# A gated FFT mixer with a token MLP: another order of token loads, layer-norm factors and sines at the start

## The chip, the cores and the metric

The kernel runs on one core of a Trainium2 chip. The metric is device time in microseconds of one execution. The core has a matrix engine (TensorE, PE in the profile), a vector engine (VectorE, DVE), a scalar engine (ScalarE, ACT), GpSimd (POOL) and a queue engine (SyncE, SP) that here only issues transfers. Each of them works through its own instructions in the order in which they were written.

## The reference

Two branches over 2048 tokens of 512 features are mixed by a gate per token.

```python
def _A_ref(x, w_r, w_i):                      # spectral branch
    X = rfft2(x.astype(float32), axes=(-2, -1)) * (w_r + 1j * w_i)
    return irfft2(X, s=(S, D), axes=(-2, -1)).astype(bfloat16)

def _B_ref(x, w1, b1, w2, b2):                # MLP over the tokens
    h = _layernorm(x, axis=-1)
    u = gelu(einsum("bsd,sf->bdf", h, w1) + b1)     # 2048 tokens -> 1792
    return (einsum("bdf,fs->bds", u, w2) + b2).transpose(0, 2, 1)

g = sigmoid((x * gate_w).sum(-1, keepdims=True))
return g * _A_ref(x, ...) + (1 - g) * _B_ref(x, ...)
```

All inputs are bf16. Both branches read the same x.

## The kernel before, in words

The tokens lie in 16 blocks of 128 (one token of a block per partition). `load_x` (line 89) brings blocks of x into `xa` and `xb`, `load_w1a` (line 92) the matching 128 rows of the first 1024 columns of w1 into `w1a`. Both are issued on SP, in the order written in lines 118 to 142. The program has eight semaphores for such transfers and takes them in turn, so that an issue waits until the transfer eight before it has landed.

The layer norm of a block needs its mean and variance. `bstat` (line 245) makes the statistics of one block on VectorE, `bn_aggr` the mean and variance `mv`. For blocks 0 and 1 the factor `rstd` comes from a square root on ScalarE (line 299) and a reciprocal on VectorE (line 302). For the others `aggr` (line 251) adds the epsilon on VectorE or on GpSimd and raises to the power of -0.5 on GpSimd (line 258). Blocks 0 to 5 are normalized on VectorE (`norm_dve`, line 270). Blocks 6 to 15 are normalized on ScalarE in pairs (`norm`, line 260), with the product of mean and factor, `nmr`, made before on VectorE (blocks 6, 7, 14, 15) or GpSimd (the others). The normalized blocks are `hn`.

TensorE first runs eight dummy matmuls on a tile of zeros (line 240). Then it takes the blocks in order: `mm1` (line 274) multiplies block b of `w1a` with block b of `hn` for eight column tiles of w1, and sums over b in eight banks. The first twelve blocks go block by block, the last four column tile by column tile, and a `gelu` on ScalarE follows each finished column tile. After that `products` (line 453) yields the remaining matmuls of the MLP one by one: the other six column tiles of w1 (line 458) and the second product with w2 (line 468). The transforms of the spectral branch (`token`, `dpass`, `inverse`) are put between them; the functions `fill`, `fill_to` and `spent` place them by a written clock in us (`T_TA` = 42.7 and so on, line 24).

The transforms need tables of sines. VectorE and ScalarE make the angles (`md`, `ma`, `mc`), VectorE masks them to a power of two (`mask`, `angles_a`), ScalarE takes the sines (`sines_d`, `sines_a`) into `TD` and `TA`, and two transposing transfers on SP make `TI` and `TB` of them. `gprod` (line 278) multiplies x with the gate weights on VectorE, and `gacc` sums the products on ScalarE. Functions that ScalarE takes from different tables (square root, sine, gelu) need a table load between them, and a one-element activation into `sink` pulls such a load forward.

The order of the norms and of the sines on each engine is that of the loops in lines 296 to 334.

Of the kernel before, what the change touches and what calls it, by code (L numbers as in the profile page):

```python
# [12 lines left out]
F32 = mybir.dt.float32  # L13
I32 = mybir.dt.int32

P = 128
S = 2048
D = 512
NB = 16
# [3 lines left out]
NDVE = 6  # L23
# [20 lines left out]
def kernel(  # L44
# [13 lines left out]
    nc = tc.nc  # L58
# [5 lines left out]
    small = ctx.enter_context(tc.tile_pool(name="small", bufs=1))  # L64
# [3 lines left out]
    def H(i, shape, name, dt=BF16):  # L68
        return big.tile(shape, dt, tag=f"h{i}", name=name)
# [11 lines left out]
    xv = A_x[0].rearrange("(b a) d -> a b d", a=P)  # L81
    w1v = B_w1.rearrange("(b a) f -> a b f", a=P)
    w2v = B_w2.rearrange("(ft f) s -> f ft s", f=P)
    xh = [H(0, [P, 8, D], "xa"), H(1, [P, 8, D], "xb")]
# [4 lines left out]
    def load_x(b0, b1):  # L89
        nc.sync.dma_start(out=xh[b0 // 8][:, b0 % 8:(b1 - 1) % 8 + 1], in_=xv[:, b0:b1])  # L90

    def load_w1a(b0, b1):
        nc.sync.dma_start(out=w1a[b0 // 4][:, b0 % 4:(b1 - 1) % 4 + 1], in_=w1v[:, b0:b1, 0:FT1 * P])
# [8 lines left out]
    def gather_w(i):  # L102
        w = (A_w_r, A_w_i)[i]
        for o, src, idx in ((wn[:, i, 8:16].rearrange("p e l -> p (e l)"), w.rearrange("(c e) l -> c (e l)", e=8), 0),
                            (wn[:, i, 16], w, 1)):
            nc.gpsimd.indirect_dma_start(out=o, out_offset=None, in_=src,
                                         in_offset=bass.IndirectOffsetOnAxis(ap=widx[:, idx:idx + 1], axis=0))
# [13 lines left out]
    nc.scalar.dma_start(out=brow[:], in_=B_b1.rearrange("(ft f) -> ft f", f=P))  # L121
    load_w1a(0, 1)
    load_x(1, 2)
    for b in range(1, 3):
        load_x(b + 1, b + 2)
        load_w1a(b, b + 1)
    load_x(4, 6)
    load_w1a(3, 4)
    load_x(6, 8)
    load_w1a(4, 6)  # L130
    load_x(8, 12)
    load_w1a(6, 8)
    load_x(12, 16)
    load_w1a(8, 12)
    gwb = small.tile([P, D], BF16, name="gwb")
    nc.sync.dma_start(out=gwb[:], in_=gate_w[None, :].to_broadcast([P, D]))
    nc.sync.dma_start(out=brow2[:], in_=B_b2.rearrange("(b a) -> b a", a=P))
# [21 lines left out]
    def iota(dst, pattern, base, cm=0):  # L159
        nc.gpsimd.iota(dst, pattern=pattern, base=base, channel_multiplier=cm,  # L160
                       allow_small_or_imprecise_dtypes=True)
# [19 lines left out]
    def gather_rows():  # L181
        gp = nc.gpsimd
        iota(widx[:, 0:1], [[0, 1]], 255, -2)
        gp.tensor_scalar(wf[:, 0:1], acol[:, 0:1], 63.5, 1016.0, op0=Alu.is_ge, op1=Alu.mult)
        gp.tensor_scalar(wf[:, 1:2], acol[:, 0:1], 0.5, -1024.0, op0=Alu.is_lt, op1=Alu.mult)
        gp.tensor_scalar(wf[:, 2:3], acol[:, 0:1], -16.0, 2048.0, op0=Alu.mult, op1=Alu.add)
        gp.tensor_add(wf[:, 0:1], wf[:, 0:1], wf[:, 1:2])
        gp.tensor_add(wf[:, 0:1], wf[:, 0:1], wf[:, 2:3])
        gp.tensor_copy(widx[:, 1:2], wf[:, 0:1])
# [4 lines left out]
    def mask(m, n):  # L194
        nc.vector.tensor_single_scalar(m, m, n - 1, op=Alu.bitwise_and)

    def nsin(dst, m, n):
        nc.scalar.activation(dst, m, ActF.Sin, bias=c_mpi, scale=2.0 * PI_IN / n)

    def psin(dst, m, n):  # L200
        nc.scalar.activation(dst, m, ActF.Sin, bias=c_pi, scale=-2.0 * PI_IN / n)
# [5 lines left out]
    def sines_d():  # L207
        nsin(TD[:, :, 1], md[:, 1], 1024)
        nsin(TD[:, :, 2], md[:, 0], 1024)
        psin(TD[:, :, 0], md[:, 0], 1024)  # L210

    def angles_a(v):
        mask(ma[v][:], 2048)
        if v == 0:
            mask(mc[:], 2048)

    def sines_a(v):
        if v == 1:
            nsin(TA[:, :, 1], ma[1][:], 2048)
        else:  # L220
            nsin(TA[:, :, 2], ma[0][:], 2048)
            psin(TA[:, :, 0], ma[0][:], 2048)
            nsin(TA[:, 0, 2, 0:1], mc[:], 2048)
            psin(TA[:, 0, 0, 0:1], mc[:], 2048)


    stats = small.tile([P, NB, nc.vector.BN_STATS_DIM], F32, name="stats")
    mv = small.tile([P, NB, nc.vector.BN_AGGR_DIM], F32, name="mv")
# [16 lines left out]
    def bstat(b):  # L245
        nc.vector.bn_stats(out=stats[:, b, :], in_=xh[b // 8][:, b % 8, :])  # L246

    def on_dve(b):
        return b <= NDVE or b == NB - 2

    def aggr(b0, b1):
        for b in range(b0, b1):
            nc.vector.bn_aggr(out=mv[:, b, :], in_=stats[:, b, :])
        eng = nc.vector if on_dve(b0) else nc.gpsimd
        eng.tensor_scalar(mv[:, b0:b1, 1], mv[:, b0:b1, 1], 1e-5, 0.0, op0=Alu.add, op1=Alu.add)  # L255
        if not on_dve(b0):
            nc.gpsimd.tensor_scalar(nmr[:, b0:b1], mv[:, b0:b1, 0], -1.0, 0.0, op0=Alu.mult, op1=Alu.add)
        nc.gpsimd.tensor_tensor(rstd[:, b0:b1], mv[:, b0:b1, 1], c_mhalf.to_broadcast([P, b1 - b0]), op=Alu.pow)  # L258

    def norm(b0, b1):  # L260
        if not on_dve(b0):
            nc.gpsimd.tensor_mul(nmr[:, b0:b1], nmr[:, b0:b1], rstd[:, b0:b1])
        else:
            nc.vector.scalar_tensor_tensor(nmr[:, b0:b1], mv[:, b0:b1, 0], -1.0, rstd[:, b0:b1],  # L264
                                           op0=Alu.mult, op1=Alu.mult)
        for b in range(b0, b1):
            nc.scalar.activation(hn[:, b, :], xh[b // 8][:, b % 8, :], ActF.Identity,  # L267
                                 bias=nmr[:, b:b + 1], scale=rstd[:, b:b + 1])

    def norm_dve(b):  # L270
        nc.vector.tensor_scalar(hn[:, b, :], xh[0][:, b, :], mv[:, b, 0:1], rstd[:, b:b + 1],
                                op0=Alu.subtract, op1=Alu.mult)
# [5 lines left out]
    def gprod(q):  # L278
        nc.vector.tensor_mul(prod[q // 2][:, 4 * (q % 2):4 * (q % 2) + 4],
                             xh[q // 2][:, 4 * (q % 2):4 * (q % 2) + 4],  # L280
                             gwb[:, None, :].to_broadcast([P, 4, D]))
# [5 lines left out]

    sink = small.tile([P, 1], F32, name="sink")
    nc.scalar.activation(sink[:], consts[:, 5:6], ActF.Sqrt, bias=consts[:, 5:6], scale=1.0)
    for v in range(2):  # L290
        nc.vector.tensor_scalar(md[:, v], lrow[:], acol[:, 1:2], 768.0 * v, op0=Alu.mult, op1=Alu.add)


    bcol = small.tile([P, NFT + NB], F32, name="bcol")
    b1f, b2f = bcol[:, 0:NFT], bcol[:, NFT:]
    for b in range(2):
        bstat(b)
        nc.vector.bn_aggr(out=mv[:, b, :], in_=stats[:, b, :])
        nc.scalar.activation(rstd[:, b:b + 1], mv[:, b, 1:2], ActF.Sqrt, bias=consts[:, 5:6], scale=1.0)
        if b == 0:  # L300
            nc.scalar.copy(b1f, pb[:, 0:NFT])
        nc.vector.reciprocal(rstd[:, b:b + 1], rstd[:, b:b + 1])
        norm_dve(b)
    bstat(2)
    nc.scalar.activation(sink[:], consts[:, 2:3], ActF.Sin, bias=c_mpi, scale=0.0)
    for v in range(2):
        nc.scalar.activation(ma[v][:], krow[:], ActF.Identity, bias=consts[:, 3 + v:4 + v], scale=acol[:, 0:1])
    nc.scalar.activation(mc[:], acol[:, 0:1], ActF.Identity, bias=consts[:, 4:5], scale=1024.0)


    aggr(2, 3)
    for b in range(2, NDVE):
        bstat(b + 1)
        norm_dve(b)
        if b + 1 < NDVE:
            aggr(b + 1, b + 2)
    for b in range(NDVE, NB, 2):
        if b > NDVE:
            bstat(b)
        if b == NDVE + 2:  # L320
            norm(b - 2, b)
            sines_d()
        bstat(b + 1)
        aggr(b, b + 2)
        if b == NDVE:
            mask(md[:], 1024)
        if b == NB - 2:
            angles_a(1)
        if b > NDVE:
            norm(b, b + 2)  # L330
        if b == NB - 6:
            angles_a(0)
            sines_a(0)
    sines_a(1)
    for b in range(12):
        for ft in range(FT1):
            mm1(b, ft)
    for q in range(4):
        gprod(q)
    gather_rows()  # L340
    gather_w(0)
    gather_w(1)
# [4 lines left out]
                                in_=TD[:].rearrange("p s t k -> p (s t k)"))  # L347
    nc.sync.dma_start_transpose(out=TB[:].rearrange("p s t k -> p (s t) k"),
                                in_=TA[:].rearrange("p s t k -> p (s t k)"))
# [445 lines left out]
    b = NB - 1  # L795
# [36 lines left out]
```

## Time and profile before

| what | value |
|---|---|
| median of 3 runs | 129.32 us (128.65, 129.32, 130.08) |
| the profiled execution's own time | 128.63 us |
| its span in the profile | 126.7 us |
| TensorE busy | 122.3 us, 97% |
| VectorE busy | 111.6 us, 88% |
| ScalarE busy | 89.7 us, 71% |
| GpSimd busy | 39.6 us, 31% |
| granted TensorE clock, mean | 0.995 |
| transfers | 24.05 MB, mean 190 GB/s |
| first matmul of the first product | 4.82 us |
| last evacuation on VectorE | 123.37 us |

The span reaches from the program's first instruction to its last one; 1.9 us of the execution's time lie outside it. Busy times are sums over the span. A busy TensorE is not the same as a TensorE at its full rate, since its matmuls overlap in the pipeline: the distance from one matmul's end to the next one's tells the rate.

### The profile page before, as it was taken

The page shows a single profiled execution, that of the slowest core. Times are in us where ns is not written, and L with a number is a line of the kernel's source. Part 1 is how long each engine was busy: PE and PEld are TensorE (multiplying, and loading weights), DVE is VectorE, ACT ScalarE, POOL GpSimd, SP SyncE. Part 2 cuts the span into 40 slices and gives each one's busy share as a digit, 9 for nine tenths or more (in the row PEclk, how much of TensorE's full clock was granted, in tenths as well). Part 3 has the DMA queues.
Part 4 walks back from the last instruction along what each step waited for, and adds up shares of the span by engine and source line. Part 5 has one row for each costly group of instructions (what it writes and reads, how often), then busy time and mean ns, then how long its engine had stood idle before and what let it go on. Part 6 is the DMA issues. An engine that isn't in the chain of part 4 may idle for free.

```text
span 126.7 us, 2074 instructions
## 1 busy us (share of the span) xinstructions
PE 122.3 (97%) x750; PEld 65.2 (51%) x750; DVE 111.6 (88%) x190; ACT 89.7 (71%) x137; POOL 39.6 (31%) x67
## 2 busy tenths in 40 slices
PE   6999999999999999999999999999999999999990
PEld 2244444444444576557764765477644444444480
DVE  4799998999999999999999999999999999993140
ACT  4391299999897699998994799229785599522420
POOL 7133288998887198000040000000000000261200
PEclk9999999999999999999999999999999999999998
DMA  3899999998899999999579206710021101269991
GB/s 95 268 327 379 368 374 352 292 309 262 206 276 121 320 290 293 290 287 291 143 220 294 65 0 190 228 42 0 0 79 50 41 3 41 83 82 201 175 224 29
DMA packets 34635, 24.05 MB, mean 190 GB/s; under 512 B 5536, under 2 KB 32032, under 8 KB 34624
## 3 DMA queue, kind: packets, MB, share of 16 engines
q1 hardware_dynamic: 32516, 21.02, 60.4%
q0 software_dynamic: 1936, 2.76, 13.0%
q8 instruction: 6, 0.10, 0.3%
q10 hardware_dynamic: 172, 0.13, 0.3%
q14 instruction: 5, 0.04, 0.1%
HBM read 19.15 MB, written 3.67 MB: 180 GB/s over the span
## 4 chain that ended last, share of the span: by engine, by line
PE 97%; DVE 0%; issue 0%
PE yb L468 36%; PE u L275 22%; PE u L458 16%; PE ivt L657 5%; PE ivd L673 3%; PE pw L240 3%; PE dp L525 3%; PE yb L800 2%; PE tok L516 2%; PE tok L517 2%; PE ivt L651 0%; PE tok L513 0%; DVE tbv L802 0%; DVE warm L145 0%; PE pb L239 0%
## 5 line engine op out<-in xcount | busy, mean ns | idle before, releaser
L468 PE MATMUL yb<-gl,w2t 128*128 128x512 bf16 x210 | 47.4, 379 | 0.0
L468 PEld LDWEIGHTS <-w2t 128*128 128x128 bf16 x210 | 20.2, 98 | 22.1
L275 PE MATMUL u<-hn,w1a 128*128 128x512 bf16 x128 | 28.5, 385 | 0.0
L458 PE MATMUL u<-hn,w1b 128*128 128x512 bf16 x96 | 23.3, 379 | 0.0
L448 ACT ACTIVATE tbv<-yb,ombb,omg 128x512 bf16<-128x512 f32 x15 | 11.6, 775 | 15.3 <-PE yb L468 15.1
L275 PEld LDWEIGHTS <-w1a 128*128 128x128 bf16 x128 | 12.7, 99 | 15.9 <-issue 1.5
L778 POOL DMA_DIRECT2D out_dram<-ap x3 | 4.0, 1528 | 49.2 <-DVE ap L773 45.3
L458 PEld LDWEIGHTS <-w1b 128*128 128x128 bf16 x96 | 9.0, 98 | 8.0
L286 ACT ACTIVATE junk<-prod 128x512 bf16<-128x512 bf16 x16 | 10.1, 631 | 0.3
L354 ACT ACTIVATE gl<-u,bcol 128x512 bf16<-128x512 f32 x14 | 9.2, 688 | 1.3 <-PE u L458 0.8
L629 ACT CAST R<-ivt 128x1024 bf16<-128x1024 f32 x8 | 7.8, 1038 | 2.3 <-PE ivt L657 2.3
L258 POOL TENSOR_TENSOR rstd<-mv,consts 128x2 f32<-128x2 f32 (+1 forms) x9 | 6.3, 703 | 8.1 <-DVE mv L255 8.0
L629 ACT CAST H<-ivd 128x1024 bf16<-128x1024 f32 x7 | 6.9, 1047 | 0.8 <-PE ivd L673 0.8
L787 DVE TENSOR_TENSOR tbv<-tbv,ap 128x512 bf16<-128x512 bf16 x3 | 1.3, 425 | 5.5 <-ACT tbv L448 5.5
L246 DVE BATCH_NORM_STATS2 stats<-xa 128x6 f32<-128x512 bf16 x8 | 5.5, 686 | 0.5 <-DMA xa<-in_A_x_dram 0.5
L267 ACT ACTIVATE hn<-xb,nmr,rstd 128x512 bf16<-128x512 bf16 x8 | 5.8, 802 | 0.0
L547 DVE TENSOR_TENSOR tatb<-PMA,wn 128x1024 bf16<-128x1024 bf16 x8 | 5.0, 690 | 0.2 <-issue 0.2
L246 DVE BATCH_NORM_STATS2 stats<-xb 128x6 f32<-128x512 bf16 x8 | 5.2, 676 | 0.0
L267 ACT ACTIVATE hn<-xa,nmr,rstd 128x512 bf16<-128x512 bf16 x2 | 1.5, 804 | 5.1 <-DVE nmr L264 5.1
L673 PEld LDWEIGHTS <-R 128*128 128x128 bf16 x64 | 3.8, 98 | 2.5 <-ACT R L629 2.5
L547 DVE TENSOR_TENSOR tatb<-PMB,wn 128x2048 bf16<-128x2048 bf16 x4 | 4.7, 1226 | 0.2
L518 ACT CAST ZA<-tok 128x1024 bf16<-128x1024 f32 x4 | 4.0, 1019 | 1.4 <-PE tok L517 1.3
(198 smaller groups left out, 225.8 us busy)
## 6 DMA issues: line engine op xcount, KB each, us to landing
w2t<-in_B_w_dram SPq DMA_DIRECT2D x8, 896.0 KB, 9.8
w1b<-in_B_w_dram SPq DMA_DIRECT2D x3, 1024.0 KB, 16.3
w1a<-in_B_w_dram SPq DMA_DIRECT2D x2, 1024.0 KB
out_dram<-tbv SPq DMA_DIRECT2D x14, 128.0 KB, 4.0
out_dram<-ap POOLq DMA_DIRECT2D x3, 512.0 KB, 6.8
w1a<-in_B_w_dram SPq DMA_DIRECT2D x4, 256.0 KB, 4.4
w1a<-in_B_w_dram SPq DMA_DIRECT2D x2, 512.0 KB, 8.0
xb<-in_A_x_dram SPq DMA_DIRECT2D x2, 512.0 KB, 7.3
```

Source lines behind the costliest of these rows:

```text
L246: nc.vector.bn_stats(out=stats[:, b, :], in_=xh[b // 8][:, b % 8, :])
L267: nc.scalar.activation(hn[:, b, :], xh[b // 8][:, b % 8, :], ActF.Identity, bias=nmr[:, b:b + 1], scale=rstd[:, b:b + 1])
L275: nc.tensor.matmul(u1[ft], lhsT=w1a[b // 4][:, b % 4, ft * P:(ft + 1) * P], rhs=hn[:, b, :], start=(b == 0), stop=(b == NB - 1))
L286: nc.scalar.activation(junk[:], prod[b // 8][:, b % 8], ActF.Copy, accum_out=glog[:, b:b + 1])
L354: nc.scalar.activation(gl[:, ft, :], src, ActF.Gelu_apprx_tanh, bias=b1f[:, ft:ft + 1], scale=1.0)
L448: nc.scalar.activation(tbv[0][:, b], y[:], ActF.Identity, bias=gate["ombb2"][:, b:b + 1], scale=gate["omg"][:, b:b + 1])
L458: nc.tensor.matmul(u[:], lhsT=w1b[c][:, b, k * P:(k + 1) * P], rhs=hn[:, b, :], start=(b == 0), stop=(b == NB - 1))
L468: nc.tensor.matmul(y[:], lhsT=w2t[b // 2][:, ft, (b % 2) * P:(b % 2 + 1) * P], rhs=gl[:, ft, :], start=(ft == 0), stop=(ft == NFT - 1))
L547: mul(tt[:, i, :, r:r + n], PM[:, 2 * s:2 * s + 2, r:r + n], w[:, None].to_broadcast([P, 2, n, 256]))
L629: nc.scalar.copy(out, pr[:].rearrange("p h n -> p (h n)"))
L657: nc.tensor.matmul(o[:, 2 * v:2 * v + 2], lhsT=UV[:, 2 * v + c, r, par::2], rhs=TB[:, s, c:c + 2], start=(c == 0), stop=(c == 1))
L673: nc.tensor.matmul(pr[:, c, o * P:(o + 1) * P], lhsT=plane(par, cos), rhs=TI[:, lst, t], start=True, stop=True)
```

## The change

It rearranges the first 30 us and leaves the rest as it is.

- Token block 2 is issued on ScalarE's queue, behind the square-root table load. SP's list loses that issue, and from block 4 on weight blocks are issued one by one, and tokens 8 to 11 in two pairs.
- Block 2's factor is made like those of 0 and 1, with the root on ScalarE. The statistics of block 3 are taken in two halves of 256 features into a tile `st3`; the first half stands between block 2's root and its reciprocal.
- Blocks 6 and 7 get their factors one at a time instead of as a pair. Block 7's now goes through GpSimd.
- The norms of 8 and 9 stand ahead of the short sines, and those of 14 and 15 ahead of the long ones; the latter stand behind the first gate product in VectorE's order. The mask of `md` moves behind the statistics of 8 and 9.

```diff
     load_w1a(0, 1)
     load_x(1, 2)
-    for b in range(1, 3):
-        load_x(b + 1, b + 2)
-        load_w1a(b, b + 1)
+    load_w1a(1, 2)
+    load_x(3, 4)
+    load_w1a(2, 3)
     load_x(4, 6)
     load_w1a(3, 4)
     load_x(6, 8)
-    load_w1a(4, 6)
-    load_x(8, 12)
-    load_w1a(6, 8)
+    load_w1a(4, 5)
+    load_w1a(5, 6)
+    load_x(8, 10)
+    load_w1a(6, 7)
+    load_x(10, 12)
+    load_w1a(7, 8)
     load_x(12, 16)
-    load_w1a(8, 12)
+    load_w1a(8, 10)
+    load_w1a(10, 12)
...
     def aggr(b0, b1):
         for b in range(b0, b1):
-            nc.vector.bn_aggr(out=mv[:, b, :], in_=stats[:, b, :])
+            nc.vector.bn_aggr(out=mv[:, b, :], in_=stats[:, b, :] if b != 3 else st3[:])
...
     nc.scalar.activation(sink[:], consts[:, 5:6], ActF.Sqrt, bias=consts[:, 5:6], scale=1.0)
+    nc.scalar.dma_start(out=xh[0][:, 2], in_=xv[:, 2])
...
+    st3 = small.tile([P, 2, nc.vector.BN_STATS_DIM], F32, name="st3")
+
+    def bstat3(h):
+        nc.vector.bn_stats(out=st3[:, h, :], in_=xh[0][:, 3, 256 * h:256 * h + 256])
+
-    for b in range(2):
+    for b in range(3):
         bstat(b)
...
+        if b == 2:
+            bstat3(0)
         nc.vector.reciprocal(rstd[:, b:b + 1], rstd[:, b:b + 1])
         norm_dve(b)
-    bstat(2)
...
-    aggr(2, 3)
-    for b in range(2, NDVE):
+    bstat3(1)
+    aggr(3, 4)
+    for b in range(3, NDVE):
         bstat(b + 1)
         norm_dve(b)
-        if b + 1 < NDVE:
-            aggr(b + 1, b + 2)
-    for b in range(NDVE, NB, 2):
-        if b > NDVE:
-            bstat(b)
-        if b == NDVE + 2:
-            norm(b - 2, b)
-            sines_d()
+        aggr(b + 1, b + 2)
+    bstat(NDVE + 1)
+    norm(NDVE, NDVE + 1)
+    aggr(NDVE + 1, NDVE + 2)
+    norm(NDVE + 1, NDVE + 2)
+    for b in range(NDVE + 2, NB, 2):
+        bstat(b)
         bstat(b + 1)
         aggr(b, b + 2)
-        if b == NDVE:
+        if b == NDVE + 2:
             mask(md[:], 1024)
         if b == NB - 2:
             angles_a(1)
-        if b > NDVE:
+        if b < NB - 2:
             norm(b, b + 2)
+        if b == NDVE + 2:
+            sines_d()
         if b == NB - 6:
             angles_a(0)
-            sines_a(0)
-    sines_a(1)
...
     for q in range(4):
         gprod(q)
+        if q == 0:
+            norm(NB - 2, NB)
+            sines_a(0)
+            sines_a(1)
```

## The prediction

> **What bounds the kernel now.** I read the page's busy shares and the chain that ended last, then the stretches of the first product's matmuls, and then each engine's order of time over the first 34 us, which is all that the change touches.
>
> ```profile
> PE 122.3 (97%) x750; PEld 65.2 (51%) x750; DVE 111.6 (88%) x190; ACT 89.7 (71%) x137; POOL 39.6 (31%) x67
> ...
> PE 97%; DVE 0%; issue 0%
> ```
>
> The chain never leaves TensorE once it has started, so a change in the other engines' order is worth only the holes that it closes in TensorE's row, or costs the holes that it opens.
>
> ```profile
> 4.82 28.50 PE L275 MATMUL u<-hn,w1a 128*128 128x512 bf16 x128
> ...
> 4.80:6.10 1.30, 1.28 (x4) 0.45 (x4) 1.00 0.88 275
> 6.10:15.70 9.60, 9.60 (x46) 4.40 (x45) 1.00 1.05 358
> 15.70:16.30 0.60, 0.60 (x4) 0.19 (x2) 1.00 1.02 375
> 16.30:33.30 17.00, 17.00 (x79) 7.54 (x77) 1.00 1.04 294
> ```
>
> The first line is the whole first product, the others count its matmuls by stretch. In the trace's single records consecutive ends are 0.216 us apart, and 128 x 0.216 is 27.6 us, against 28.50. The 0.9 us between them are: three matmuls at the start that end 0.42 us apart (0.6 us together), one gap of 0.304 instead of 0.216 us at the 49th matmul (15.89 us; 0.09 us), and 0.16 us by which a single matmul (0.379) is longer than the step. Block b starts with matmul 8b+1. So the 49th is the first of block 6, and the whole loss that depends on the order of work is 0.09 us there. From 33.3 us on the chain shows no wait at all up to the last evacuation at 123.37 us.
>
> Why block 6 is late, and how near the other blocks are:
>
> ```profile
> 6.47 0.69 DVE L246 BATCH_NORM_STATS2 stats<-xa 128x6 f32<-128x512 bf16 x1
> 8.27 0.41 DVE L271 TENSOR_SCALAR hn<-xa,mv,rstd 128x512 bf16<-128x512 bf16 x1
> 9.63 0.42 DVE L271 TENSOR_SCALAR hn<-xa,mv,rstd 128x512 bf16<-128x512 bf16 x1
> 22.04 0.16 DVE L264 SCALAR_TENSOR_TENSOR nmr<-mv,rstd 128x2 f32<-128x2 f32 x1 [0.58 <-POOL rstd L258]
> ...
> 15.03 1.52 ACT L267 ACTIVATE hn<-xa,nmr,rstd 128x512 bf16<-128x512 bf16 x2 [5.06 <-DVE nmr L264]
> 28.51 3.80 ACT L354 ACTIVATE gl<-u,bcol 128x512 bf16<-128x512 f32 x6
> ```
>
> Columns are start and duration in us; the bracket is idle time before and what ended it. Row 5: ScalarE sits 5.06 us until block 6's factor is there and ends that block at 15.83 us; its matmul, due at 15.80, starts at 15.89. That is the 0.09. Rows 2 and 3: blocks 2 and 3 are normalized at 8.68 and 10.05 us; their matmuls start at 8.89 and 10.62 us. With the 0.06 us that lie between readiness and start at block 6, the margins are 0.15 and 0.51 us. Block 1 has 0.55, block 8 (ready 18.75, due 19.28) about 0.5.
>
> ```profile
> 1.66 0.90 SPq L90 DMA_DIRECT2D xa<-in_A_x_dram  x2
> 2.60 0.43 SPq L93 DMA_DIRECT2D w1a<-in_B_w_dram  x1
> ...
> xa<-in_A_x_dram SPq DMA_DIRECT2D x4, 128.0 KB, 3.0
> ```
>
> Token blocks 1 and 2 are issued together; an issue takes SP 0.43 to 0.47 us with its gap. In the trace's landing records block 2 (issued at 2.13) lands at 6.07 us, weight block 1 (issued at 2.60) at 6.73, token block 3 at 7.10. VectorE reads block 2 at 6.47: 0.4 us of margin.
>
> **The change part by part.**
>
> *Third tokens on ScalarE's queue.* SP loses one issue, so weight block 1 and all behind it go out 0.47 us sooner. The new issue stands behind the square-root table load and its one-element activation, which end at 3.00 us. If ScalarE's sequencer runs ahead of that work it goes out at about 1.5 us, otherwise at 3.0. ScalarE's one early issue in the trace (the 14x128 bias) took 0.65 us; ending at 3.65 it is before the first root, which waits for VectorE until 3.83. I take 3.0. Landing: the first tile took 2.14 us from issue to landing with nothing ahead of it, block 2 itself 3.94 us behind SP's backlog. So 5.1 to 6.9 us; I take 6.2, and VectorE at 6.47 does not wait. Cost 0; bounds 0 and 0.2 us (6.94-6.47 less the 0.26 us of margin at block 3, below).
>
> This rests on how two queues share the engines. The Trainium skill, DMA: Bandwidth & Descriptors, section Queues, rings and completion order, says that each DMA engine takes turns between the queue rows that it has work for; by that rule block 2 shares with SP's backlog and the sum is unchanged. No run here shows two loaded hardware queues at once. The same page (Issuing engines are not separate DMA queues) speaks against expecting more: a second engine saves only the issue time.
>
> *Third root on ScalarE, fourth sums in halves.* Block 2's factor now goes statistics 6.47-7.16, aggregate to 7.38, root on ScalarE (0.29 us) to 7.71, reciprocal (0.16) and normalization. In the root's shadow VectorE does half of block 3's statistics; 256 instead of 512 elements is about 0.4 us by the 0.69 of a whole one, ending at 7.80. Reciprocal to 8.0, normalization 8.02-8.43: 0.25 us earlier than 8.68. The second half (0.4), aggregate (0.18), epsilon (0.15) and the power on GpSimd (0.58) put block 3 at 10.30: 0.25 us later than 10.05, margin 0.26. The loop of one block (8.88 to 10.24) stays 1.36 us, so blocks 4 and 5 are at 11.67 and 13.03, 0.14 to 0.28 later, against 12.29 and 14.01 us at which they are due. Cost on TensorE 0. The Sin table load and the angle products behind it move back by about 1.8 us, to an end near 11.8 us; nothing reads them before 15 us.
>
> *Seventh and eighth factors singly.* Block 6 no longer waits for the statistics of 7: aggregate, epsilon to 13.32, power to about 13.85, nmr 14.0, ScalarE 14.05 to 14.86. It is 0.97 us earlier and the 0.09 hole closes. Block 7 now goes alone through GpSimd's four instructions; the same four took 1.43 to 1.92 us for pairs (17.91 to 19.34 and 15.90 to 17.82), so from 14.15 it is ready for ScalarE at 15.6 to 16.1 and done at 16.4 to 16.9, due at 17.46. Blocks 8 and 9 follow on GpSimd at 15.7 to 17.2-17.7, block 8 is done at 18.0 to 18.5, due at 19.2.
>
> *Last norms ahead of the sines.* VectorE: statistics of 8 start at 14.13 as before (14.15), the md mask (0.46) moves behind them, and by the old rows' steps the last epsilon is at 21.08, the last mask to 21.71. Then the first gate product (1.14 from issue to issue) fills the time in which VectorE waited 0.58 us for GpSimd's power; the products end near 26.35, 0.3 us before the old 26.65. That matters, since VectorE then runs on to 83.5 us with one hole of 0.19, and its last plane there is due on TensorE at 83.87. ScalarE: from block 8 on it has 1.46 + 1.52 (three short sines) + 4.4 (six blocks) + 3.6 (long sines) + 1.29 (table) = 12.3 us without a stop, so the gelus begin at 29.5 to 30.0 instead of 28.51. The first next-product matmul (33.15 us) needs the bank that the fourth gelu frees: at 0.63 us each, 32.0 to 32.5. Hidden, margin 0.6 to 1.1; without that cover each us late costs one us. The gate sums on ScalarE are late by under a us and regain it in its holes of 0.79 (40.48) and 1.30 us (44.59).
>
> *Weights by blocks.* Three more issues on SP, 1.4 us, and each waits for the transfer eight before it, as now (the issue at 6.09 stands on block 2's landing). At the tightest wait the seven still in flight are 1.7 MB, over 4 us at the 375 GB/s of the third stretch above, so the engines stay fed. Weights 4 and 8 land before their partners instead of with them (11.87 and 18.9 now, due at 12.3 and 19.3). The gate weights go out 3 us later but queue behind the same bytes, packets over by 19.5 now, needed at 21.7. Cost 0.
>
> *Sum.* 126.73 less 0.09 is 126.6 us of span, with the same 1.9 us around it 128.5 us for an execution like the profiled one (128.63). That one is the fastest shown; the median is 129.32, 0.7 above it. What fills the 0.7 no trace shows. The change widens the smallest margins (block 6 from -0.09 to 0.8, block 2 from 0.15 to 0.4), so I take another 0.1 off there: 129.32 - 0.09 - 0.1 = 129.1 us.
>
> The 0.6 us of slow first matmuls is a term that varies: they end 0.42 us apart until 6.05 us. The Trainium skill, TensorE: Matmul & The Clock Gate (Part 1), says that the full clock is granted after a free-running window, so that the cold part changes from run to run; the trace's switch 5.07 us after the first dummy matmul fits that, and by it the change does nothing to this term.
>
> **The rivals.**
>
> *Third tokens land late (slower).* ScalarE's issue may be late, or the engines may serve the backlog first. For: landing lags the last packet already (block 2's end at 5.27, its landing is 6.07). Against: only 0.9 MB is queued on SP by 3.0 us. It decides from 6.73 us on, 6.47 plus block 3's margin of 0.26; each us later stops TensorE and VectorE alike. Behind everything issued by then it lands about where weight block 2 does now, 7.75: +1.0 us, 130.1. For over 1% it would have to land after 8.2.
>
> *ScalarE late at the gelus (slower).* If GpSimd's four instructions for 8 and 9 run into VectorE's mask (its last multiply took 0.65 instead of 0.20 in such a place) and block 10 waits too, the fourth gelu passes 33.15; a us past the margin gives 129.9.
>
> *More holes than the profiled run shows (faster).* If the 0.7 us between profile and median are late landings in the first 16 us, the wider margins take most of it: 128.4. Against: the three margins shrink elsewhere (block 3 from 0.51 to 0.26).
>
> *No effect.* VectorE's row, gapless to 83.5 us, holds TensorE at 83.87 whatever comes earlier: 129.3. It lies within the forecast's own range.
>
> **How the numbers follow.** Forecast with no effect, 128.6 to 129.6: 0.57. Tokens late 0.19, gelus late 0.10, more holes closed 0.14. 1% is 1.29 us, about what a measurement of this kernel can tell from no change. Under 128.03 us lies half of the faster case (0.07) and 0.03 of the forecast by the scatter of three runs (128.65 to 130.08): 0.10. Over 130.61 lie 0.08 of late tokens, 0.05 of late gelus and 0.03 of scatter: 0.16. Range 128.1 to 130.8, the low end by the faster case, the high end by the slower ones with the scatter on top.
>
> **What would show it.** Right: the 49th matmul 0.216 us after the 48th; the issue on ScalarE's queue at or before 3.0 us and no wait on a DMA before block 2's statistics; block 2 done near 8.4, block 3 near 10.3, block 6 near 14.9; the products' last row near 26.3; the first gelu near 29.7 and no step over 0.216 at 33.15. Wrong: a wait of VectorE on xa over 0.3 us, a hole in the first product after block 2, or a gap before the first matmul of line 458 (33.15 us).

## The result and the profile after

The changed kernel takes 129.20 us (median of 22 runs), the kernel before 128.73 us (median of 22 runs): a ratio of 1.0031, with a 95% interval of 1.0016 to 1.0047. It is slower by 0.47 us in the medians. The three runs shown before had a median of 129.32, 0.6 us above that of 22 runs; the forecast of 129.1 was 0.2 us under it.

The busy shares and the chain of the changed kernel (the page's parts 1 and 4):

```profile
PE 121.2 (95%) x737; PEld 65.0 (51%) x750; DVE 111.7 (88%) x191; ACT 89.9 (71%) x138; POOL 39.7 (31%) x70
...
PE 73%; ACT 10%; DVE 6%; POOL 3%; DMA 3%; issue 2%; SPq 1%
```

Before, the chain was 97% TensorE. Now it leaves TensorE and runs through ScalarE, VectorE, GpSimd and a transfer: up to some point in the first product TensorE is no longer what ends last. The order of time on TensorE shows the point, and the list of waits names what was waited for (us in total, times, longest):

```profile
27.68 2.11 PE L279 MATMUL u<-hn,w1a 128*128 128x512 bf16 x9
30.46 3.61 PE L279 MATMUL u<-hn,w1a 128*128 128x512 bf16 x16 [0.68 <-ACT gl L369]
...
ACT hn L271 <- POOL nmr L266: 1.6, 2, 0.9
...
PE u L279 <- ACT gl L369: 0.7, 1, 0.7
...
PE u L279 <- DVE hn L275: 0.6, 2, 0.3
```

The matmul at 30.46 us is the 113th, since 16 are left of 128. The one before it started at 29.404, so it was due at 29.62 and lost 0.84 us (the bracket's 0.68 counts from the modelled end of the matmul before). It is the first of column tile 1 in the last four blocks, and it waited for a gelu. ScalarE's order of time shows which one:

```profile
1.42 1.28 ACT L293 ACT_TABLE_LOAD   x1 [1.42 <-PEq L831]
1.49 0.37 ACTq L294 DMA_DIRECT2D xa<-in_A_x_dram  x1
...
14.43 0.81 ACT L271 ACTIVATE hn<-xa,nmr,rstd 128x512 bf16<-128x512 bf16 x1 [2.33 <-DVE nmr L268]
15.91 0.81 ACT L271 ACTIVATE hn<-xa,nmr,rstd 128x512 bf16<-128x512 bf16 x1 [0.67 <-POOL nmr L266]
17.66 1.52 ACT L271 ACTIVATE hn<-xb,nmr,rstd 128x512 bf16<-128x512 bf16 x2 [0.93 <-POOL nmr L266]
...
29.73 0.69 ACT L369 ACTIVATE gl<-u,bcol 128x512 bf16<-128x512 f32 x1
```

The first gelu, that of tile 0, ends at 30.42, and 0.04 us later tile 1 starts. Before, it ended at 29.20 with tile 1 starting at 29.70: 0.45 us of room, given the same 0.04. The two tiles have different banks of PSUM, the memory into which matmuls sum. But they are halves of one memory tile of two banks, a PSUM pair (`pu[0]` holds column tiles 0 and 1). Among the matmuls of these four blocks the first of column tiles 1, 3 and 5, the second halves of the three pairs, carries a wait on ScalarE that the others of its tile do not; column tile 7, with a bank of its own, has none. That fits waits that the program sets per memory tile and not per bank. The fence also shows two idle times of ScalarE, 0.67 and 0.93 us, that the kernel before did not have, and the issue on ScalarE's queue at 1.49 us, while the table load ran.

VectorE at the start, the first line before the change and the others after it:

```profile
4.68 0.69 DVE L246 BATCH_NORM_STATS2 stats<-xa 128x6 f32<-128x512 bf16 x1
...
5.01 0.69 DVE L250 BATCH_NORM_STATS2 stats<-xa 128x6 f32<-128x512 bf16 x1 [0.24 <-DMA xa<-in_A_x_dram]
...
8.28 0.41 DVE L275 TENSOR_SCALAR hn<-xa,mv,rstd 128x512 bf16<-128x512 bf16 x1
...
10.16 0.41 DVE L275 TENSOR_SCALAR hn<-xa,mv,rstd 128x512 bf16<-128x512 bf16 x1
```

Block 1's statistics, which started at 4.68 us before, now wait for their transfer until 5.01. Blocks 2 and 3 are ready at 8.69 and 10.57 us; I had 8.43 and 10.30.

### The profile page after: what moved, and what is told of

The parts are those of the page before. It is cut to its first block, busy times and chain, and to the rows that moved or that the text cites. A ratio compares the mean times of both kernels' runs of the same rounds, so it can differ in the third digit from the quotient of the medians.

```text
span 127.4 us, 2068 instructions
## 1 busy us (share of the span) xinstructions
PE 121.2 (95%) x737; PEld 65.0 (51%) x750; DVE 111.7 (88%) x191; ACT 89.9 (71%) x138; POOL 39.7 (31%) x70
## 4 chain that ended last, share of the span: by engine, by line
PE 73%; ACT 10%; DVE 6%; POOL 3%; DMA 3%; issue 2%; SPq 1%
PE yb L483 35%; PE u L473 16%; PE ivt L672 5%; ACT hn L271 4%; PE ivd L688 3%; PE u L279 3%; PE dp L540 3%; DMA xa<-in_A_x_dram 3%; PE yb L815 2%; PE tok L531 2%; PE tok L532 2%; POOL rstd L262 2%; DVE stats L250 2%; ACT TA L202 2%; DVE hn L275 2%
## 5 line engine op out<-in xcount | busy, mean ns | idle before, releaser
L483 PE MATMUL yb<-gl,w2t 128*128 128x512 bf16 x203 | 46.4, 379 | 0.4
L473 PE MATMUL u<-hn,w1b 128*128 128x512 bf16 x92 | 22.6, 379 | 0.2
L262 POOL TENSOR_TENSOR rstd<-mv,consts 128x1 f32<-128x1 f32 (+1 forms) x9 | 6.0, 664 | 8.5 <-DVE mv L259 8.5
L250 DVE BATCH_NORM_STATS2 stats<-xa 128x6 f32<-128x512 bf16 x7 | 4.8, 686 | 0.7 <-DMA xa<-in_A_x_dram 0.7
L688 PE MATMUL ivd<-TI,R 128*128 128x128 bf16 x64 | 4.9, 220 | 0.0
```

The source lines that it names most:

```text
L473: nc.tensor.matmul(u[:], lhsT=w1b[c][:, b, k * P:(k + 1) * P], rhs=hn[:, b, :], start=(b == 0), stop=(b == NB - 1))
L483: nc.tensor.matmul(y[:], lhsT=w2t[b // 2][:, ft, (b % 2) * P:(b % 2 + 1) * P], rhs=gl[:, ft, :], start=(ft == 0), stop=(ft == NFT - 1))
L688: nc.tensor.matmul(pr[:, c, o * P:(o + 1) * P], lhsT=plane(par, cos), rhs=TI[:, lst, t], start=True, stop=True)
```

## The experiments

Two theories were at odds. A: the loss is tile 1's wait for tile 0's gelu, because ScalarE comes 1.2 us later to it. B: VectorE's chain, late from block 1 on, holds TensorE anyway, and the gap only shows the loss there. Ratios below are to the kernel before, from the same chip, with 95% intervals.

**Tile order in the changed kernel.**

```diff
-    for ft in (0, 2, 4, 6, 1, 3, 5, 7):
+    for ft in (0, 2, 4, 6, 7, 1, 3, 5):
```

> The changed kernel, with the last four blocks' column tiles taken in the order 0, 2, 4, 6, 7, 1, 3, 5 instead of 0, 2, 4, 6, 1, 3, 5, 7; ScalarE gets the same work. Theory A: tile 1 shares a PSUM pair with tile 0, so its first matmul waits for the first gelu (ends 30.42 us, matmul due at 29.62, starts 30.46: 0.84 us). With tile 7 between, tile 1 is due 0.86 us later, the gap at the 113th matmul closes, and about 0.8 us of the 129.2 go: 128.4 to 128.5. Rival B: VectorE's chain, late by 0.33 us from the second token block on, holds TensorE at the second inverse (83 to 84 us) whatever is closed earlier: the gap moves there, under 0.2 us gained, 129.0 or more.

128.18 us, ratio 0.9946 (0.9920 to 0.9973). TensorE and ScalarE around the place:

```profile
27.64 5.99 PE L279 MATMUL u<-hn,w1a 128*128 128x512 bf16 x27
...
30.13 4.74 ACT L369 ACTIVATE gl<-u,bcol 128x512 bf16<-128x512 f32 x8
```

27 matmuls in one piece, though the gelus start at 30.13, later still than in the changed kernel. From 1.0031 to 0.9946 is 0.85%, or 1.1 us; the two intervals leave 0.4 to 1.3%, which holds the 0.84 us of the gap (0.65%). B falls, since it allowed 0.2 us: what this gap took was gained at the end. The room is small: in this profile the first gelu ends at 30.82 us and tile 1 starts at 30.88.

**The tile order alone, on the kernel before** (the same two lines).

> Control: the kernel before with only the tile order 0, 2, 4, 6, 7, 1, 3, 5. Theory A: the kernel before has no gap at tile 1 (its first gelu ends 0.4 us ahead), so the order alone brings nothing: ratio 1.000 within 0.2%. Rival: the order helps by itself (banks freed sooner for the next products), and what the two runs of the changed kernel with this order gained is not the closed gap: 0.4% or more faster.

128.90 us, ratio 1.0002 (0.9986 to 1.0018). Where there is no gap to close the order is worth nothing, within 0.2%. So the 0.54% that the run above gains over the kernel before is to be looked for in the rest of the change. The smaller transfers alone are worth 0.2% of it (below); where the remainder comes from no run shows.

**A dose of lateness on the kernel before.**

```diff
     sines_a(1)
+    sines_a(1)
     for b in range(12):
```

> The kernel before with the last long sine on ScalarE done twice (1.04 us more ahead of the gelu's table load; same output). Theory A: its first gelu ends at 29.2 us with tile 1 due at 29.70, so 0.45 us of the delay is hidden and 0.6 us shows as a gap at the 113th matmul: about 0.6 us slower than the kernel before. The deadline that I had used (fourth gelu before 33.15 us) has 2.1 us to spare: by it, no change.

The gap appears where expected:

```profile
30.50 3.61 PE L275 MATMUL u<-hn,w1a 128*128 128x512 bf16 x16 [0.57 <-ACT gl L355]
```

From start to start it is 0.95 instead of 0.216 us, 0.73 lost. The time is 129.06 us, 0.26 above the median of the kernel before, and the ratio of 1.0007 (0.9982 to 1.0031) does not settle a cost. The gap is shown; that it costs its length is not. The 12 runs lie between 128.99 and 129.23, far closer together than those of the kernel before. Waits that come and go ahead of this gap would be absorbed in it; that fits the narrow spread, but no run tests it.

**The same dose with the tile order** (both edits).

> The kernel before with the last long sine done twice, as in the run before (0.73 us of gap at the 113th matmul), and with the column tiles in the order 0, 2, 4, 6, 7, 1, 3, 5. Theory A (the wait is tile 1's on tile 0's gelu, through their shared PSUM pair): the 113th matmul is then tile 7's and waits for nothing, tile 1 is due 0.86 us later: no gap, the same time as the kernel before, 128.8, though ScalarE does 1.04 us more. Rival: TensorE would be held at its next bank by any ScalarE delay: still 0.5 us or more slower than without the extra sine.

```profile
27.81 5.99 PE L275 MATMUL u<-hn,w1a 128*128 128x512 bf16 x27
...
PEld L275 <- DMA w1a<-in_B_w_dram: 1.0, 2, 0.8
PE u L275 <- DMA w1a<-in_B_w_dram: 0.3, 1, 0.3
```

No gap at tile 1, 128.85 us, ratio 0.9988 (0.9971 to 1.0005): 1.04 us more of ScalarE work costs nothing that the interval shows. The wait is this tile's, not ScalarE's load. In time, though, the two runs with the dose lie only 0.19% apart, inside their intervals; the price of a gap rests on the runs of the changed kernel. The two lines with a transfer are new: in this execution weights 8 to 11 landed at 19.77 us, and TensorE lost 0.48 us at block 8, due at 19.34. This is a loss of the kernel before that its profile (landing at 18.91) had not shown.

**Weights and tokens 4 to 11 in smaller transfers, on the kernel before** (the SP list of the change, with token block 2 left on SP).

> The kernel before with only weights 4 to 11 and tokens 8 to 11 issued in smaller transfers; token block 2 stays on SP. In three profiles weights 8 to 11 landed at 18.9, 19.0 and 19.8 us and are due at 19.25: in the last one TensorE waited 0.48 us at block 8. Theory C: the smaller transfers bring weights 8 and 9 in at 16.7 us, the wait at block 8 goes, 0.1 to 0.3 us off the median and fewer executions above 129 us. Rival: the late landing is rare and the median does not move.

128.65 us, ratio 0.9980 (0.9965 to 0.9995): 0.2% or about 0.25 us gained. Weights 8 and 9 land at 17.3, 10 and 11 at 18.9 us. A part of the change that I had costed at nothing is thus a gain, and the slowest of its 12 runs is 128.90.

**All changed transfers on the kernel before, token block 2 on ScalarE's queue.**

```diff
     nc.scalar.activation(sink[:], consts[:, 5:6], ActF.Sqrt, ...)
+    nc.scalar.dma_start(out=xh[0][:, 2], in_=xv[:, 2])
```

> The kernel before with only the changed order of transfers (token block 2 on ScalarE's queue, weights singly). Theory A': block 1's statistics start at 5.0 to 5.4 instead of 4.7, block 6 is normalized 0.3 to 0.6 us later, the hole at the 49th matmul grows from 0.09 to 0.4 to 0.7, and the first gelu follows: 0.3 to 0.5 us slower, 129.1 to 129.3. My prediction's view (landings have margin): no change, 128.8.

128.87 us, ratio 0.9993 (0.9975 to 1.0010): not slower, so the expectation of 0.3 to 0.5 us failed, and the prediction's "no change" holds for the sum of all transfers. The mechanism is there, in smaller size:

```profile
4.95 0.69 DVE L250 BATCH_NORM_STATS2 stats<-xa 128x6 f32<-128x512 bf16 x1 [0.17 <-DMA xa<-in_A_x_dram]
...
PE u L279 <- DVE hn L275: 0.6, 3, 0.2
```

The hole at block 6 is 0.25 us (0.471 from start to start) instead of 0.09. But the run above, with block 2 on SP, has one of the same size (0.465), so this hole does not tell the queue's part. That part shows at block 2, for which TensorE waited 0.40 us here and 0.05 there, and in the start of the 49th matmul, at 16.17 against 15.99 us. Beside the run above the issue on ScalarE's queue costs about 0.13% (0.9993 less 0.9980), inside the intervals of both.

**Token block 2 back on SP, in the changed kernel.**

> The changed kernel with token block 2 back on SP's queue behind block 1. Theory A': the issue on ScalarE's queue went out at 1.49 us, ahead of block 1's, and took its share: block 1 landed at 4.99 instead of 4.40 us, VectorE's statistics of block 1 moved from 4.68 to 5.01, and all factors and so the first gelu came 0.33 us later. Back on SP: statistics of block 1 at 4.7, first gelu's end near 30.1 instead of 30.42, the gap before tile 1 near 0.5 instead of 0.84: 0.3 us less, 128.9. Rival: ScalarE's lateness comes only from its waits on GpSimd for blocks 7 and 8, and the start has no part in it: first gelu's end within 0.1 us of 30.42, 129.2.

129.02 us, ratio 1.0014 (0.9986 to 1.0042). The first gelu ends at 30.17 instead of 30.42 and the gap is 0.24 instead of 0.84 us, partly because this execution's first matmuls ran slow, which makes tile 1 due at 30.0. The direction is as expected; the time alone does not tell it from no effect.

**The short sines ahead of the norms of 8 and 9, in the changed kernel.**

```diff
+        if b == NDVE + 2:
+            sines_d()
         if b < NB - 2:
             norm(b, b + 2)
-        if b == NDVE + 2:
-            sines_d()
```

> The changed kernel with the three short sines ahead of the norms of 8 and 9 on ScalarE again (VectorE's order untouched, the mask is done at 16.3 us). Theory A: they fill the 0.93 us that ScalarE waits for GpSimd's factor of block 8 (16.72 to 17.66), so the first gelu starts near 28.8 and ends near 29.5, before tile 1 is due at 29.62; the gap closes without any change in TensorE's order: 128.4 to 128.5. Block 8 would be ready at 19.04 us, due at 19.2, a hole of at most 0.1 there. Rival: the gelus are late for the long sines that now stand behind the norms of 14 and 15, not for that wait: first gelu still near 29.7, 129.2.

128.82 us, ratio 0.9998 (0.9972 to 1.0024), and the expectation was wrong: the gap shrank to 0.65 us only.

```profile
21.69 1.52 ACT L271 ACTIVATE hn<-xb,nmr,rstd 128x512 bf16<-128x512 bf16 x2 [0.18 <-POOL nmr L266]
23.57 1.52 ACT L271 ACTIVATE hn<-xb,nmr,rstd 128x512 bf16<-128x512 bf16 x2 [0.36 <-DVE nmr L268]
...
29.89 4.21 ACT L369 ACTIVATE gl<-u,bcol 128x512 bf16<-128x512 f32 x7
```

The 0.93 us were filled, but ScalarE then ran into the next norms before GpSimd and VectorE had supplied their factors. The second bracket is the factor that now stands behind the first gate product on VectorE. After those norms come 3.6 us of long sines and the table load, all of which stand ahead of the first gelu. In this execution block 1 was also late: its statistics started at 5.37 us.

**All sines as before, in the changed kernel** (the edit above, and the first long angle set back between the norms of 11 and 12).

> The changed kernel with the short sines ahead of the norms of 8 and 9 and the two sines and two single elements of the first angle set between the norms of 11 and 12, as in the kernel before; tile order as in the changed kernel. The run with the short sines alone left ScalarE waiting 0.18 us for block 10 and 0.36 us for block 14. Theory B': what makes the gelus late is that ScalarE is given norms that GpSimd and VectorE have not supplied yet while sines that are ready stand behind them; with all sines as before only block 7's wait of 0.67 us stays: first gelu's end near 29.6 instead of 30.42, gap under 0.3 us, 128.4. Rival: block 7's way through GpSimd is enough to make it late: gap 0.5 or more, 128.8.

128.67 us, ratio 0.9964 (0.9941 to 0.9987). TensorE has 36 matmuls in one piece there:

```profile
25.71 7.93 PE L279 MATMUL u<-hn,w1a 128*128 128x512 bf16 x36
...
28.90 0.69 ACT L369 ACTIVATE gl<-u,bcol 128x512 bf16<-128x512 f32 x1
```

Only the wait of 0.67 us for block 7 is left on ScalarE, and the first gelu ends at 29.59. So the order of the sines makes the gelus late: norms that are not supplied yet stand ahead of sines that are ready. Block 7's own way through GpSimd is not enough. This run closes the gap from ScalarE's side, with TensorE's order untouched, and its ratio is 0.67% under that of the changed kernel (0.3 to 1.1% by the two intervals), about the gap's 0.84 us (0.65%). After the tile order it is the second run that finds the loss there.

**The changed kernel with the tile order and with token block 2 on SP.**

> The changed kernel with the tile order 0, 2, 4, 6, 7, 1, 3, 5 and with token block 2 back on SP. With the gap at tile 1 gone, what is left of the issue on ScalarE's queue is its effect on the start: block 1 lands at 4.3 instead of 5.0 to 5.4 us. Theory A': TensorE, which in executions with an early full clock waited 0.63 us in all for blocks 1 to 3, waits 0.2 to 0.3 less: 127.9 to 128.1 against 128.18 with the block on ScalarE's queue. Rival: the cold clock covers it: 128.2, no difference.

128.00 us, ratio 0.9937 (0.9915 to 0.9959). It has the lowest median and ratio of all versions, ahead of both kernels. Against the run with the order alone the 0.18 us are inside the intervals. Its profile, again without slow first matmuls, has waits of 0.07, 0.07 and 0.16 us for blocks 1, 2 and 3, 0.30 in all instead of the changed kernel's 0.63.

**All three edits in the changed kernel.**

> The changed kernel with all three edits: tile order 0, 2, 4, 6, 7, 1, 3, 5, token block 2 on SP, sines as in the kernel before. Theory: the run with the first two has no gap left after block 3, so the earlier gelus are worth nothing more: 128.0 within 0.2, ratio 0.993 to 0.995. Rival: ScalarE's later work (the gate sums, the transforms' copies) was still held up by the late gelus: 127.6 or less.

128.17 us, ratio 0.9950 (0.9930 to 0.9971), no further gain, as expected: without the gap earlier gelus are worth nothing. The profiles also split the lateness of the first gelu's end: 30.42 us in the changed kernel, 29.59 with the sines as before, 29.31 here with block 2 on SP as well, and 29.20 in the kernel before. By these single profiles the order of the sines made 0.83 of the 1.22 us and the issue on ScalarE's queue 0.28.

## Why the prediction was wrong, point by point

*The deadline of the gelus.* This is the step that failed. The prediction had the gelus begin "at 29.5 to 30.0 instead of 28.51", and they began at 29.73. It then took as their deadline "the bank that the fourth gelu frees" at 33.15 us, and called the delay hidden with a margin of 0.6 to 1.1 us. The deadline that decides is the end of the first gelu, needed by tile 1 at 29.62; it came at 30.42. The deadline that I had named was kept: the fourth gelu ended at 32.1, and the next product's first matmul waited for nothing. I followed who reuses a bank, and missed who shares a memory tile with it. The wait stands in the program before as well, with 0.45 us of room, and the price that I gave for missing a deadline (one us for each) is about what the tile order gave back (1.1 us for a gap of 0.84, with an interval of 0.4 to 1.3%).

*The rival "ScalarE late at the gelus"* had the right engine, with the wrong cause and place: it was held to need a collision on GpSimd, at a chance of 0.10. No collision was needed: the first norms' waits of 0.67 and 0.93 us are the plain consequence of the new order, and my own sum for ScalarE contained them.

*Third tokens on ScalarE's queue.* I took the issue at 3.0 us, behind the table load; it went out at 1.49, 0.07 us after that load began, and the block landed at 4.83 instead of my 6.2. The Trainium skill, Advanced Engine Details and Errata, section Sequencer Loop, says that the sequencer pushes an engine instruction into a queue, where it waits for its semaphores and resources; that fits a sequencer that went on to the issue while the load ran. I had expected block 2 to come late. It came early, ahead of SP's block 1 (issued at 1.66), and block 1 came late: in the five profiles with the issue on ScalarE's queue it landed at 4.93 to 5.38 us, in the profiles of the kernel before and of the same change with the block on SP at 4.2 to 4.4. VectorE's later factors moved with it: block 1's statistics started at 4.95 to 5.41 us there, against 4.68 in the kernel before, 0.3 to 0.7 us later. The Trainium skill, DMA: Bandwidth & Descriptors, section Queues, rings and completion order, has the engines take turns between queues; that fits the displaced block.

*Third root, fourth sums in halves.* The half took 0.39 to 0.42 us, as estimated, and block 3 follows block 2 by 1.88 us against 1.87 in the sum. Right in size, but all 0.26 to 0.27 us later for the reason above. In the changed kernel's profile, whose matmuls ran at full rate from the first one on, TensorE waited 0.40, 0.07 and 0.16 us for blocks 1, 2 and 3: about as much as the 0.6 us that slow first matmuls cost the kernel before. So the slow start, which I had taken as unaffected by the change, hides such waits where it occurs: the profile with the tile order has four slow matmuls and part of a fifth, and only 0.05 us of waits, at block 3.

*Seventh and eighth factors.* The hole at block 6 closed, as predicted: the matmuls around 16 us keep 0.216. Block 6 was normalized at 15.24 instead of 15.83 us.

*Last norms.* The row behind the gate products starts at 26.48 us; the sum had 26.35, the old row 26.65. VectorE's later row, the ground for "no effect", did not hold TensorE back in any profile.

*Weights by blocks.* Costed at zero; alone it gained 0.2% (0.05 to 0.35%). My guess that the 0.7 us between the profile and the median "no trace shows" were late landings has one execution behind it, and the three-run median that it was drawn from was 0.6 us above that of 22 runs.

*The chances.* 0.16 for over 1% slower and 0.74 within 1%: within 1% is what came. That the time lies 0.1 us from the forecast is luck: the median that it started from was 0.6 us too high, and the step is 0.47 us slower where 0.2 faster was forecast.

## What to carry to other kernels

When an engine's work is moved later, find the first instruction on the bounding engine that waits for it, from the list of waits in program order. Look also for waits that a shared memory tile makes between two halves that do not touch each other; ordering the work so that the halves are not neighbours can be enough. And on an engine that works in written order, look for ready work that stands behind work whose inputs are still being made: here the ready sines stood behind such norms, and setting them ahead again brought 0.83 us on ScalarE.

## What the runs showed of the hardware

The DMA issue behind the table load on ScalarE's queue did not wait for it: it went out at 1.49 us in the changed kernel, with the load from 1.42 to 2.70. The four other profiles with this issue have it at 1.48.

The slow first matmuls differ between executions of the same chip and almost the same program: none of the first product in the changed kernel's profile, three in that of the kernel before, four and part of a fifth with the tile order. The Trainium skill, TensorE: Matmul & The Clock Gate, Part 1, has the number of such matmuls vary from run to run, and these traces agree. The granted clock of the view reads 1.00 from 4.80 to 6.10 us in the kernel before, where three matmuls ended 0.42 instead of 0.216 us apart, so here the steps tell the rate and that column does not. The slow matmuls cost that kernel 0.6 us; the changed kernel had none in its profile and gained nothing by it, since its blocks were not ready.
